# A three-stage attention and MoE kernel: tiles placed in a second pool, one reduction on another engine, another prologue order

## The chip, the cores and the metric

The kernel runs on 1 core of a Trainium2 chip. The metric is the device time of one execution in microseconds (us). Before the change the median of 3 runs is 1623.13 us (1617.84 to 1623.29). Engines are named as the profile names them: PE (matmul) and PEld (its weight load), DVE (VectorE), ACT (ScalarE), POOL (GpSimd), SP (it issues DMAs).

## What is computed

Linear attention (softmax of q over its features, of k over the sequence), then two feed-forward stages. Shapes: 8 batches, 8 heads, sequence 576, head size 64; so 4608 tokens of 512; hidden sizes 1536 and 768. q, k, v are float32, the weights float64.

```python
q_s = exp(q - max(q, axis=-1));  q_s = q_s / (sum(q_s, axis=-1) + 1e-9)
k_s = exp(k - max(k, axis=2));   k_s = k_s / (sum(k_s, axis=2) + 1e-9)
kv = einsum('bhsd,bhse->bhde', k_s, v)
x = einsum('bhsd,bhde->bhse', q_s, kv)          # to (4608, 512)
x = (silu(x @ w_gate) * (x @ w_val)) @ w_out
out = maximum(maximum(x @ w1, x @ w2), x @ w3) @ w2_out
```

## The kernel before

The tokens are cut into 9 blocks of 512. Each block runs through 60 groups of matmuls: for each of 12 hidden slices G, V and O (gate, value, output; the x stage, moving operand `xhi`/`xlo`), then for each of 6 slices W1, W2, W3 and P (the y stage, moving operand `yhi`/`ylo`). A product is made of three float32r matmuls (`mm3`): high x high, high x low, low x high, where `x_split`, `split_hi` and `split_lo` make the two parts of activations and weights. A group is 12 matmuls of 512 columns, so a block has 216 matmuls with `y` moving (W1 to W3), 288 with `x` moving (G, V), and the rest with `h` or a P weight moving. In the profile's names `pm<-yhi,whi` means: `yhi` moves, `whi` is stationary.

The float64 weights are loaded once, in block 0, turned to float32 there by two ACT steps (`convert_act`, lines 462 and 463) and two DVE steps (`convert_dve`, lines 471 and 474), and kept. In block 0 the main loop asks for conversions group by group (`quota`), and for each group ACT also casts the high part (line 489). The attention of block j+1 is worked into the groups of block j at places from a table (`SLOTS`, `SLOTS_FIRST`).

The attention of block 0 has no block before it. It is a prologue, in two halves of four heads, whose steps stand in a list written by hand (`PROLOGUE`); its DMAs stand in `LOADS`. Engines run their own instructions in exactly this order. For each half: `k_max` (maxima within a partition, DVE), `k_max_all` (over the 128 partitions: `partition_all_reduce` on POOL, line 161), `k_sub`, `k_exp`, `kv0`/`kv1` (matmuls with v), `q_max`, `q_sub`, `q_exp`, `q_sum`, `q_mul`, `qt0`/`qt1` (transposes on PE and copies on ACT), `kv_scale`, `x0`/`x1` (matmul and `x_split`). A third field "P" puts a step on POOL: `q_sub` and `k_sub` of half 1 and both `q_mul`. Among them stand `act n` and `dve n` (convert until n groups are done), `hi`/`lo` (split a weight) and `mm n` (first half of group n).

All tiles come from one SBUF pool, `sb`, and stand one behind the other in the order in which the program first asks for them. `v_sb` takes 5280 bytes in a partition (10 x 512 + 160), `qm`, `qx`, `qs`, `qr`, `kr1`, `kr2` take 8 to 128. The addresses of the built program, modulo 512 bytes:

| tiles | before | after |
|---|---|---|
| `raw_*`, `kvhi`, `kvlo`, `k_sb`, `q_sb` | 128 | 128 |
| `yhi`, `ylo`, `stage`, `qt`, `qthi` | 288 | 128 |
| `xhi`, `xlo`, `whi`, `wlo`, `plain`, `s`, `h`, `hhi`, `hlo` | 416 | 128 |
| `qtlo`, `o`, `kvf` | 32 | 128 |

Of the kernel before, what the change touches and what calls it, by code (L numbers as in the profile page):

```python
# [8 lines left out]
F32 = mybir.dt.float32  # L9
# [4 lines left out]
ALU = mybir.AluOpType  # L14
AX = mybir.AxisListType
# [3 lines left out]
def linear_attention_moe_moe_kernel(  # L19
# [20 lines left out]
    nc = tc.nc  # L40
    B, H, S, D = q.shape
# [4 lines left out]
    TB = 512  # L46
    NB = NT // TB
    HH = H // 2
    HP = HH // 2
    R = 4  # L50
    SM = 128 * R
    SR = S - SM
    VC = 2 * (D + 2)

    sb = ctx.enter_context(tc.tile_pool(name="sb", bufs=1))
    dram = ctx.enter_context(tc.tile_pool(name="dram", bufs=1, space=bass.MemoryType.DRAM))
    ps = ctx.enter_context(tc.tile_pool(name="ps", bufs=1, space=bass.MemoryType.PSUM))

# [15 lines left out]
        "k": sb.tile([128, R, HH, D], F32, name="k_sb"),  # L74
        "kr": sb.tile([128, HH, D], F32, name="kr_sb"),
        "q": sb.tile([128, R, HH, D], F32, name="q_sb"),
        "v": sb.tile([128, R + 1, HP, 2, D + 2], F32, name="v_sb"),
    }


# [3 lines left out]
    w = [raw[t].rearrange("p f c n -> p (f c n)") for t in ("W1", "W2", "W3")]  # L84
    n, m = R * HH * D, HH * D
    spot = w[1][:, n + (R + 1) * HP * VC:]
    ident, ones = spot[:, 0:128], spot[:, 128:256]
    diag = spot[:, 256:512].rearrange("p (g n) -> p g n", g=HP)

    def hrd(a, i):  # L90
        return a[:, i:i + n].rearrange("p (h r d) -> p h r d", r=R, h=HH)
# [58 lines left out]
    def k_max(t, c):  # L150
# [2 lines left out]
            out=c["km"], in_=t["k"].rearrange("p r h d -> p h d r"), axis=AX.X, op=ALU.max  # L153
        )

    def k_max_all(t, c):
        nc.vector.tensor_tensor(
            out=c["km"][0:SR], in0=c["km"][0:SR], in1=t["kr"][0:SR], op=ALU.max
        )
        c["kb"] = sb.tile([128, HH, D], F32, tag="kb", name="kb")  # L160
        nc.gpsimd.partition_all_reduce(
            c["kb"].rearrange("p h d -> p (h d)"),
            c["km"].rearrange("p h d -> p (h d)"),
            128,
            bass_isa.ReduceOp.max,
        )
# [16 lines left out]

    def both(a, tag):

        o = sb.tile([128, HP, TB // 32], F32, tag=tag, name=tag)
        for i in range(4):
            p, p1 = 32 * i, 32 * (i ^ 1)
            nc.vector.tensor_copy(out=o[p:p + 32], in_=a[p1:p1 + 32])
        return o  # L190

    def q_max(t, c):
        c["qm"] = sb.tile([128, HP, TB // 32], F32, tag="qm", name="qm", bufs=2)
        nc.vector.tensor_reduce(out=c["qm"], in_=t["qp"], axis=AX.X, op=ALU.max)
        o = both(c["qm"], "qx")
        nc.vector.tensor_tensor(out=c["qm"], in0=c["qm"], in1=o, op=ALU.max)
# [8 lines left out]
        nc.scalar.activation(out=t["qp"][:, part], in_=t["qp"][:, part], func=AF.Exp)  # L205

    def q_sum(t, c):
        qs = sb.tile([128, HP, TB // 32], F32, tag="qs", name="qs")
        nc.vector.tensor_reduce(out=qs, in_=t["qp"], axis=AX.X, op=ALU.add)
        o = both(qs, "qx")  # L210
        nc.vector.scalar_tensor_tensor(out=qs, in0=qs, scalar=1e-9, in1=o, op0=ALU.add, op1=ALU.add)
        c["qr"] = qs
        nc.vector.reciprocal(out=qs, in_=qs)
# [36 lines left out]
    def first_load_v(t, hf):  # L250
        for g in range(HP):
            h0 = hf * HH + 2 * g
            for u in range(2):
                nc.sync.dma_start(
                    out=t["v"][:, 0:R, g, u, 0:D],
                    in_=v[0, h0 + u, 0:SM, :].rearrange("(p r) d -> p r d", r=R),
                )
            nc.sync.dma_start(
                out=t["v"][0:SR, R, g, :, 0:D],
                in_=v[0, h0:h0 + 2, SM:S, :].rearrange("h p d -> p h d"),  # L260
            )
# [20 lines left out]
        nc.scalar.activation(out=t["kr"][0:SR], in_=t["kr"][0:SR], func=AF.Exp)  # L282

    def first_q_max(t, c):
        c["qm"] = sb.tile([128, HH, R], F32, tag="qm", name="qm", bufs=2)
        nc.vector.tensor_reduce(out=c["qm"], in_=t["qs"], axis=AX.X, op=ALU.max)

    def first_q_sub(t, c, eng=nc.vector):
# [10 lines left out]
            )  # L299

    def first_q_sum(t, c):
        qs = sb.tile([128, R, HH], F32, tag="qs", name="qs")
        nc.vector.tensor_reduce(out=qs, in_=t["q"], axis=AX.X, op=ALU.add)
        c["qr"] = sb.tile([128, R, HH], F32, tag="qr", name="qr", bufs=2)
        nc.vector.tensor_scalar_add(qs, qs, 1e-9)
        nc.vector.reciprocal(out=c["qr"], in_=qs)

# [20 lines left out]
        x_split(px, 0, hf * HP + g)  # L328

    def kv_scale(t, c):  # L330
        r = sb.tile([128, HP, 1], F32, tag="kr1", name="kr1", bufs=2)
        nc.vector.tensor_scalar_add(r, c["pkv"][:, :, D:D + 1], 1e-9)
        c["kvr"] = sb.tile([128, HP, 1], F32, tag="kr2", name="kr2", bufs=2)
        nc.vector.reciprocal(out=c["kvr"], in_=r)
        if "kv" in t:
            c["kvf"] = [t["kv"][u * D:(u + 1) * D, :, u * D:(u + 1) * D] for u in range(2)]
        else:
            kvf = sb.tile([128, HP, D], F32, tag="kvf", name="kvf")
            c["kvf"] = [kvf[u * D:(u + 1) * D] for u in range(2)]
        for u in range(2):  # L340
            p = slice(u * D, (u + 1) * D)
            nc.vector.tensor_tensor(
                out=c["kvf"][u], in0=c["pkv"][p, :, 0:D],
                in1=c["kvr"][p].to_broadcast([D, HP, D]), op=ALU.mult,
            )
# [257 lines left out]
    def attention(j, hf, t):  # L603
# [9 lines left out]
        if new:  # L613
            at("load_k", lambda: load_k(t, b, hf))
            at("load_v", lambda: load_v(t, b, hf))
            at("k_max", lambda: k_max(t, c))
            at("k_max_all", lambda: k_max_all(t, c))
            at("k_sub", lambda: k_sub(t, c))
            for i in range(3):
                at(f"k_exp{i}", lambda i=i: k_exp(t, c, i))  # L620
            for g in range(HP):
                at(f"kv{g}", lambda g=g: kv_mm(t, c, g))
            at("kv_scale", lambda: kv_scale(t, c))
            at("kv_split", lambda: kv_split(t, c, b, hf))
# [46 lines left out]
    with tc.manual_schedule():  # L671
        c = ({}, {})
        FIRST = {
            "k_max": first_k_max, "k_max_all": k_max_all, "k_sub": first_k_sub, "k_exp": first_k_exp,
            "q_max": first_q_max, "q_sub": first_q_sub, "q_exp": first_q_exp,
            "q_sum": first_q_sum, "q_mul": first_q_mul, "kv_scale": kv_scale,
        }

        def run(name, i, *a):
            t = first[i] if i in (0, 1) else None  # L680
            if name == "act":
                converts_act(i)
            elif name == "dve":
                converts_dve(i)
            elif name == "hi":
                split_hi(i)
            elif name == "lo":
                split_lo(i)
            elif name == "load":
                loads(i)  # L690
            elif name == "mm":
                proj(i, st["x", 0], 0, KC // 2)
            elif name.startswith("load_"):
                {"k": first_load_k, "q": first_load_q, "v": first_load_v}[name[5:]](t, i)
            elif name.startswith("kv") and name[2:].isdigit():
                kv_mm(t, c[i], int(name[2:]), ("acc2", "acc3")[i])
            elif name.startswith("qt"):
                first_q_t(t, c[i], int(name[2:]))
            elif name.startswith("x"):
                first_x_mm(t, c[i], i, int(name[1:]))  # L700
            elif a and a[0] == "P":
                FIRST[name](t, c[i], nc.gpsimd)
            else:
                FIRST[name](t, c[i])

        for t in first:
            nc.gpsimd.memset(t["v"][:, :, :, :, D:D + 2], 1.0)
            nc.gpsimd.memset(t["v"][SR:128, R], 0.0)
            nc.gpsimd.memset(t["kr"][SR:128], 0.0)
        nc.gpsimd.memset(att["kr"][SR:128], 0.0)  # L710
        for name, i in LOADS:
            run(name, i)
        make_identity(nc, ident)
        for t in first:
            nc.gpsimd.memset(t["kv"], 0.0)
        for a in (*kvhi, *kvlo):
# [4 lines left out]
        for n, (j, kind, f) in enumerate(groups):  # L721
            i = n % GPB
# [67 lines left out]


LOADS = (
    ("load_k", 0), ("load_q", 0), ("load_q", 1), ("load", 1), ("load_v", 0), ("load_k", 1),
    ("load", 3), ("load_v", 1),
)
PROLOGUE = (
    ("k_max", 0), ("act", 1), ("q_max", 0), ("k_max_all", 0), ("q_sub", 0), ("q_max", 1),
    ("q_exp", 0), ("k_sub", 0), ("q_sub", 1, "P"), ("k_exp", 0), ("q_sum", 0),
    ("q_mul", 0, "P"), ("kv0", 0), ("k_max", 1), ("k_max_all", 1), ("q_exp", 1), ("act", 2),
    ("k_sub", 1, "P"), ("act", 3), ("kv1", 0), ("dve", 1), ("qt0", 0), ("kv_scale", 0), ("dve", 2),  # L800
# [4 lines left out]
)  # L805


# [30 lines left out]
```

## Time and profile before

| | |
|---|---|
| median of 3 runs | 1623.13 us (1617.84 to 1623.29) |
| the profiled execution | 1619.9 us, of which 1618.1 us are its span |
| granted TensorE clock, mean | 0.993 |
| PE busy | 1557.1 us (96%) |
| DVE, ACT, POOL busy | 939.6, 740.7, 34.2 us |
| first `pm` matmul | 56.77 us |
| blocks 1 to 6, each | about 171 us; block 0 takes 197 us from its first `pm` matmul |

The trace is read in three parts: the prologue (to 57 us), block 0 (to 254 us) and the eight blocks behind it. Matmul durations in the trace are longer than their spacing, since they are pipelined; the spacing is read from the chain of work, where a piece of n matmuls stands with its time.

### The profile page before, as it was taken

The page shows a single profiled execution, that of the slowest core. Times are in us where ns is not written, and L with a number is a line of the kernel's source. Part 1 is how long each engine was busy: PE and PEld are TensorE (multiplying, and loading weights), DVE is VectorE, ACT ScalarE, POOL GpSimd, SP SyncE. Part 2 cuts the span into 40 slices and gives each one's busy share as a digit, 9 for nine tenths or more (in the row PEclk, how much of TensorE's full clock was granted, in tenths as well). Part 3 has the DMA queues.
Part 4 walks back from the last instruction along what each step waited for, and adds up shares of the span by engine and source line. Part 5 has one row for each costly group of instructions (what it writes and reads, how often), then busy time and mean ns, then how long its engine had stood idle before and what let it go on. Part 6 is the DMA issues. An engine that isn't in the chain of part 4 may idle for free.

```text
span 1618.1 us, 19598 instructions
## 1 busy us (share of the span) xinstructions
PE 1557.1 (96%) x7300; PEld 1266.2 (78%) x7300; DVE 939.6 (58%) x1589; ACT 740.7 (46%) x1234; POOL 34.2 (2%) x40
## 2 busy tenths in 40 slices
PE   1699999999999999999999999999999999999999
PEld 1487767888888888888888888888888888888887
DVE  3487785547554765467546754575547643664343
ACT  2799873344434443344334443434443433443332
POOL 2100000000000000000000000000000000000000
PEclk9899999999999999999999999999999999999999
DMA  7485754103310322121411141023103211111100
GB/s 197 124 248 156 204 145 101 33 20 76 75 53 27 69 64 65 33 51 37 102 33 44 39 108 33 21 69 87 44 23 69 65 33 39 33 52 33 33 21 33
DMA packets 197183, 112.96 MB, mean 70 GB/s; under 512 B 145888, under 2 KB 169440, under 8 KB 197088
## 3 DMA queue, kind: packets, MB, share of 16 engines
q1 hardware_dynamic: 197088, 111.72, 25.5%
q8 instruction: 57, 0.93, 0.2%
q14 instruction: 38, 0.31, 0.1%
HBM read 97.52 MB, written 14.16 MB: 69 GB/s over the span
## 4 chain that ended last, share of the span: by engine, by line
PE 85%; ACT 7%; issue 3%; DVE 2%; POOL 1%; SPq 0%; DMA 0%; DVEq 0%; POOLq 0%; ACTq 0%
PE pm L500 58%; PE acc L500 24%; ACT stage L463 2%; ACT whi L489 1%; PE pkv L230 1%; PE px L382 1%; PE px L383 1%; PE px L381 1%; SPq L148 0%; ACT raw_w L462 0%; PE acc L530 0%; ACT plain L462 0%; ACT ring_yhi L463 0%; DVE wlo L494 0%; ACT ring_ylo L463 0%
## 5 line engine op out<-in xcount | busy, mean ns | idle before, releaser
L500 PE MATMUL pm<-xhi,whi 128*128 128x512 f32 x864 | 340.1, 394 | 4.2 <-ACT s L563 4.1
L500 PE MATMUL pm<-xlo,whi 128*128 128x512 f32 x864 | 337.8, 391 | 0.4 <-DVE xlo L394 0.4
L500 PE MATMUL pm<-xhi,wlo 128*128 128x512 f32 x864 | 337.6, 391 | 0.0
L566 DVE TENSOR_TENSOR h<-s,pm 128x512 f32<-128x512 f32 x108 | 74.2, 687 | 332.6 <-PE pm L500 330.9
L500 PE MATMUL pm<-yhi,whi 128*128 128x512 f32 x648 | 258.5, 399 | 4.5 <-ACT s L570 3.9
L500 PE MATMUL pm<-yhi,wlo 128*128 128x512 f32 x648 | 256.2, 395 | 0.0
L500 PE MATMUL pm<-ylo,whi 128*128 128x512 f32 x648 | 255.8, 395 | 0.0
L520 ACT CAST hhi<-h 128x512 fp32r<-128x512 f32 x156 | 97.5, 625 | 320.5 <-DVE h L566 210.6
L500 PEld LDWEIGHTS pm<-xhi,whi 128*128 128x128 f32 x864 | 163.0, 189 | 40.4 <-ACT s L563 5.9
L500 PEld LDWEIGHTS pm<-xlo,whi 128*128 128x128 f32 x864 | 163.0, 189 | 35.3 <-issue 1.0
L500 PEld LDWEIGHTS pm<-xhi,wlo 128*128 128x128 f32 x864 | 162.9, 189 | 34.0
L500 PE MATMUL acc<-hhi,whi 128*128 128x512 f32 x424 | 165.2, 390 | 0.0
L500 PE MATMUL acc<-hhi,wlo 128*128 128x512 f32 x424 | 165.2, 390 | 0.0
L500 PE MATMUL acc<-hlo,whi 128*128 128x512 f32 x424 | 165.1, 390 | 0.0
L500 PEld LDWEIGHTS pm<-yhi,whi 128*128 128x128 f32 x648 | 121.8, 188 | 35.5 <-ACT s L570 5.2
L563 ACT ACTIVATE s<-pm 128x512 f32<-128x512 f32 x108 | 65.3, 605 | 177.7 <-PE pm L500 177.4
L500 PEld LDWEIGHTS pm<-yhi,wlo 128*128 128x128 f32 x648 | 121.7, 188 | 29.0
L500 PEld LDWEIGHTS pm<-ylo,whi 128*128 128x128 f32 x648 | 121.8, 188 | 28.8 <-DVE ylo L584 0.4
L489 ACT CAST whi<-raw_w 128x512 fp32r<-128x512 f32 x162 | 100.8, 622 | 60.4 <-PE pm L500 46.9
L494 DVE TENSOR_TENSOR wlo<-plain,whi 128x512 fp32r<-128x512 f32 x156 | 106.8, 685 | 17.6 <-ACT whi L489 17.5
L494 DVE TENSOR_TENSOR wlo<-raw_w,whi 128x512 fp32r<-128x512 f32 x162 | 110.0, 683 | 10.3 <-ACT whi L489 10.3
L521 DVE TENSOR_TENSOR hlo<-h,hhi 128x512 fp32r<-128x512 f32 x156 | 108.0, 692 | 12.6 <-ACT hhi L520 0.7
(146 smaller groups left out, 1957.4 us busy)
## 6 DMA issues: line engine op xcount, KB each, us to landing
plain<-kept_o SPq DMA_DIRECT2D x96, 256.0 KB, 2.6
plain<-kept_p SPq DMA_DIRECT2D x48, 256.0 KB, 2.8
out_dram<-o SPq DMA_DIRECT2D x36, 256.0 KB, 2.0
stage<-in_moe_w_dram SPq DMA_DIRECT2D x17, 512.0 KB, 3.8
v_sb<-in_v_dram SPq DMA_DIRECT2D x60, 128.0 KB, 2.9
k_sb<-in_k_dram SPq DMA_DIRECT2D x56, 128.0 KB, 3.4
stage<-in_moe_w_out_dram SPq DMA_DIRECT2D x12, 512.0 KB, 4.1
stage<-in_moe_w_gate_dram SPq DMA_DIRECT2D x6, 512.0 KB, 5.0
```

What stands on the lines that cost most here:

```text
L230: nc.tensor.matmul(out=c["pkv"][u * D:(u + 1) * D, g, :], lhsT=lhsT, rhs=rhs, start=i == 0, stop=i == R,)
L381: nc.tensor.matmul(out=px[:, a:e], lhsT=hi, rhs=qhi, start=True, stop=False)
L382: nc.tensor.matmul(out=px[:, a:e], lhsT=hi, rhs=qlo, start=False, stop=False)
L383: nc.tensor.matmul(out=px[:, a:e], lhsT=lo, rhs=qhi, start=False, stop=True)
L463: nc.scalar.activation(out=bits, in_=low, func=AF.Copy, scale=2.0 ** -29 * (1.0 - 2.0 ** -7), bias=-0.44)
L489: nc.scalar.copy(out=hi, in_=plain[n])
L494: nc.vector.tensor_tensor(out=lo, in0=plain.pop(n), in1=hi, op=ALU.subtract)
L500: nc.tensor.matmul(out=o, lhsT=a, rhs=b, start=first and m == 0, stop=last and m == 2)
L520: nc.scalar.copy(out=hi, in_=h)
L521: later.append(lambda: nc.vector.tensor_tensor(out=lo, in0=h, in1=hi, op=ALU.subtract))
L563: nc.scalar.activation(out=st["s"], in_=p, func=AF.Silu)
L566: nc.vector.tensor_tensor(out=h, in0=st["s"], in1=p, op=ALU.mult)
```

## The change

A second pool, `small`, takes `v_sb` and the small tiles, and stands behind `sb`; so everything in `sb` begins at 128 modulo 512 (the table above). `k_max_all` of block 0 becomes `first_k_max_all`, on DVE alone: transpose in blocks of 32 x 32, reduce, exchange between the four groups of 32 partitions in two rounds, spread, transpose back. The v loads of block 0 are issued by ACT instead of SP. The identity for the transposes is made first on POOL. `LOADS` and `PROLOGUE` stand in another order, and no step has the field "P" any more. Behind the prologue every engine has the same instructions in the same order as before.

```diff
     sb = ctx.enter_context(tc.tile_pool(name="sb", bufs=1))
+    small = ctx.enter_context(tc.tile_pool(name="small", bufs=1))
...
-        "v": sb.tile([128, R + 1, HP, 2, D + 2], F32, name="v_sb"),
+        "v": small.tile([128, R + 1, HP, 2, D + 2], F32, name="v_sb"),
...
+    def first_k_max_all(t, c):
+        km = c["km"].rearrange("p h d -> p (h d)")
+        nc.vector.tensor_tensor(out=c["km"][0:SR], in0=c["km"][0:SR], in1=t["kr"][0:SR], op=ALU.max)
+        kt = sb.tile([128, HH * D], F32, tag="kb", name="kt")
+        nc.vector.transpose(out=kt, in_=km)
+        top = small.tile([128, HH * D // 32], F32, tag="qm", name="top", bufs=2)
+        nc.vector.tensor_reduce(
+            out=top, in_=kt.rearrange("p (j b) -> p j b", b=32), axis=AX.X, op=ALU.max
+        )
+        for step in (1, 2):
+            o = small.tile([128, HH * D // 32], F32, tag="qx", name="qx")
+            for i in range(4):
+                p, p1 = 32 * i, 32 * (i ^ step)
+                nc.vector.tensor_copy(out=o[p:p + 32], in_=top[p1:p1 + 32])
+            nc.vector.tensor_tensor(out=top, in0=top, in1=o, op=ALU.max)
+        nc.vector.tensor_copy(
+            out=km.rearrange("p (j b) -> p j b", b=32),
+            in_=top.unsqueeze(2).to_broadcast([128, HH * D // 32, 32]),
+        )
+        nc.vector.transpose(out=kt, in_=km)
+        c["kb"] = kt.rearrange("p (h d) -> p h d", h=HH)
...
-        c["qm"] = sb.tile([128, HP, TB // 32], F32, tag="qm", name="qm", bufs=2)
+        c["qm"] = small.tile([128, HP, TB // 32], F32, tag="qm", name="qm", bufs=2)
...
-                nc.sync.dma_start(
+                nc.scalar.dma_start(
                     out=t["v"][:, 0:R, g, u, 0:D],
...
-            "k_max": first_k_max, "k_max_all": k_max_all, "k_sub": first_k_sub, "k_exp": first_k_exp,
+            "k_max": first_k_max, "k_max_all": first_k_max_all, "k_sub": first_k_sub, "k_exp": first_k_exp,
...
+        make_identity(nc, ident)
         for t in first:
             nc.gpsimd.memset(t["v"][:, :, :, :, D:D + 2], 1.0)
...
-    ("load_k", 0), ("load_q", 0), ("load_q", 1), ("load", 1), ("load_v", 0), ("load_k", 1),
-    ("load", 3), ("load_v", 1),
+    ("load_k", 0), ("load_k", 1), ("load_v", 0), ("load_q", 0), ("load", 1), ("load_q", 1),
+    ("load_v", 1), ("load", 3),
...
-    ("k_max", 0), ("act", 1), ("q_max", 0), ("k_max_all", 0), ("q_sub", 0), ("q_max", 1),
+    ("k_max", 0), ("k_max_all", 0), ("k_sub", 0), ("k_exp", 0), ("k_max", 1), ("k_max_all", 1),
```

POOL behind its memsets, before (`raw_w_65`, `raw_w_66`, `raw_w_67` are `raw_w1`, `raw_w2`, `raw_w3`, in which the prologue keeps its data; a row ISA without operands precedes a change of the kind of work on POOL):

```order
L161 ISA
L161 ISA kb<-km 128x256
L289 ISA
L289 TENSOR_TENSOR raw_w_66<-raw_w_66,qm 128x1024
L309 TENSOR_TENSOR q_sb<-q_sb,qr 128x1024
L161 ISA
L161 ISA kb<-km 128x256
L270 ISA
L270 TENSOR_TENSOR raw_w_65<-raw_w_65,kb 128x1024
```

The same place on POOL now (`raw_w_69` and `raw_w_70` are `raw_w2` and `raw_w3`):

```order
masks.py:197 MEMSET raw_w_69 128x128
masks.py:199 ISA
masks.py:199 AFFINE_SELECT raw_w_69<-raw_w_69 128x128
L732 MEMSET v_sb 128x20x2
L733 MEMSET v_sb 64x264
```

Behind these only memsets follow until the all-reduces of the later blocks: the two of block 0 and the four elementwise steps have left POOL, and the identity stands ahead of the memsets of v.

DVE at the program's start, before:

```order
L266 TENSOR_TENSOR k_sb<-raw_w_65 128x4x2x64
L267 TENSOR_TENSOR km<-k_sb 128x256
L286 TENSOR_REDUCE qm<-raw_w_65 128x16
L157 TENSOR_TENSOR km<-km,raw_w_67 64x256
L289 TENSOR_TENSOR raw_w_65<-raw_w_65,qm 128x1024
L286 TENSOR_REDUCE qm<-raw_w_66 128x16
L270 TENSOR_TENSOR raw_w_65<-raw_w_65,kb 128x1024
```

and now:

```order
L290 TENSOR_TENSOR k_sb<-raw_w_68 128x4x2x64
L291 TENSOR_TENSOR km<-k_sb 128x256
L160 TENSOR_TENSOR km<-km,raw_w_70 64x256
L162 STREAM_TRANSPOSE kt<-km 128x256
L164 TENSOR_REDUCE top<-kt 128x8
L171 COPY qx<-top 32x8 x4
L172 TENSOR_TENSOR top<-top,qx 128x8
```

The pair of L171 and L172 comes once more, then one copy of 128 x 256 that spreads the maxima, the transpose back and `k_sub`. The q steps of half 0 have moved behind the k steps of both halves, and the maxima over partitions stand where DVE waited for POOL.

ACT at the program's start, before:

```order
L462 ACT_TABLE_LOAD
L462 ACTIVATE raw_g<-stage 128x512
L463 ACTIVATE stage<-stage 128x512
L297 ACTIVATE q_sb<-raw_w_65 128x512 x2
L279 ACTIVATE k_sb<-raw_w_65 128x512 x2
L282 ACTIVATE raw_w_67<-raw_w_67 64x256
```

and now:

```order
L278 DMA raw_w_69<-in_v_dram 128x4x64 x2
L282 DMA raw_w_69<-in_v_dram 64x2x64
L303 ACT_TABLE_LOAD
L303 ACTIVATE k_sb<-raw_w_68 128x512 x2
L306 ACTIVATE raw_w_70<-raw_w_70 64x256
L321 ACTIVATE q_sb<-raw_w_68 128x512 x2
L347 COPY qt<-pt 128x512 x2
L486 ACTIVATE raw_g<-stage 128x512
L487 ACTIVATE stage<-stage 128x512
```

Twelve DMA issues (the last three are shown) now stand ahead of ACT's first instruction, k's exponentials ahead of q's, and the first conversion behind the copies of the transposed q.

## Rows read from the trace of the kernel before

**Rows 1.** The page, part 1: busy us (share of the span) and instructions by engine.

```profile
PE 1557.1 (96%) x7300; PEld 1266.2 (78%) x7300; DVE 939.6 (58%) x1589; ACT 740.7 (46%) x1234; POOL 34.2 (2%) x40
```

**Rows 2.** Windows of block 0: busy us by engine, granted clock, DMA share, GB/s.

```profile
57.00:195.00 138.00, 129.49 (x552) 98.78 (x551) 105.70 (x187) 134.08 (x182) 1.08 (x1) 0.96 0.67 198
195.00:254.00 59.00, 55.45 (x256) 40.20 (x254) 49.97 (x93) 37.67 (x56) 1.27 (x1) 1.00 0.49 130
```

**Rows 3.** Timeline of POOL in the prologue: start us, us, instruction, idle before.

```profile
13.42 0.28 POOL masks.py:199 TENSOR_SCALAR_AFFINE_SELECT raw_w<-raw_w 128x128 f32<-128x128 f32 x1 [10.61 <-issue]
...
22.87 1.08 POOL L161 PARTITION_ALL_REDUCE kb<-km  x1 [6.79 <-issue]
31.67 1.89 POOL L289 TENSOR_TENSOR raw_w<-raw_w,qm 128x1024 f32<-128x1024 f32 x1 [7.72 <-issue]
...
41.66 1.08 POOL L161 PARTITION_ALL_REDUCE kb<-km  x1 [6.23 <-issue]
49.62 2.33 POOL L270 TENSOR_TENSOR raw_w<-raw_w,kb 128x1024 f32<-128x1024 f32 x1 [6.89 <-issue]
```

**Rows 4.** Timeline: DVE's first work, transposes of half 0 on PE, ACT's table load for Silu.

```profile
5.19 0.69 DVE L266 TENSOR_TENSOR k_sb<-raw_w 128x512 f32<-128x512 f32 x1 [5.19 <-DMA raw_w<-in_k_dram]
...
35.48 1.97 PE L319 MATMUL pt<-raw_w,q_sb 128*128 128x128 f32 x8 [7.01 <-POOL q_sb L309]
...
66.12 1.28 ACT L563 ACT_TABLE_LOAD   x1
```

**Rows 5.** The chain of work in block 8: start us, us, piece.

```profile
1449.47 10.88 PE pm L500 x48
...
1547.39 16.79 PE pm L500 x72
...
1608.69 5.49 PE acc L500 x24
```

**Rows 6.** Groups of PE by shape, 850 us to the end: busy us, mean ns.

```profile
L500 PE MATMUL pm<-xhi,whi 128*128 128x512 f32 x396 | 154.3, 390 | 0.0
...
L500 PE MATMUL pm<-yhi,whi 128*128 128x512 f32 x360 | 142.8, 397 | 0.0
...
L500 PE MATMUL acc<-hlo,whi 128*128 128x512 f32 x204 | 79.5, 390 | 0.0
...
L382 PE MATMUL px<-qtlo,kvhi 128*128 128x512 f32 x4 | 1.6, 396 | 0.0
L381 PE MATMUL px<-qthi,kvhi 128*128 128x512 f32 x4 | 1.6, 394 | 0.0
```

**Rows 7.** Groups of DVE by shape, whole span: busy us, mean ns, idle before.

```profile
L494 DVE TENSOR_TENSOR wlo<-raw_w,whi 128x512 fp32r<-128x512 f32 x162 | 110.0, 683 | 10.3 <-ACT whi L489 10.3
...
L364 DVE STREAM_TRANSPOSE whole<-q_sb 128x512 f32<-128x512 f32 x32 | 22.5, 704 | 0.0
...
L216 DVE TENSOR_TENSOR q_sb<-q_sb,qs 128x1024 f32<-128x1024 f32 x16 | 19.5, 1218 | 0.0
...
L471 DVE TENSOR_SCALAR stage<-stage 128x512 uint32<-128x512 uint32 x41 | 17.4, 425 | 24.1 <-ACT stage L463 23.9
...
L189 DVE COPY qx<-qm 32x32 f32<-32x32 f32 x64 | 11.1, 173 | 1.2
...
L157 DVE TENSOR_TENSOR km<-km,kr_sb 64x256 f32<-64x256 f32 x14 | 5.8, 411 | 0.0
```

**Rows 8.** Groups of ACT by shape, whole span: busy us, mean ns, idle before.

```profile
L489 ACT CAST whi<-raw_g 128x512 fp32r<-128x512 f32 x108 | 66.6, 617 | 0.0
...
L463 ACT ACTIVATE stage<-stage 128x512 uint16<-128x512 uint32 x41 | 55.9, 1364 | 1.3
...
L462 ACT ACTIVATE raw_g<-stage 128x512 f32<-128x512 f32 x6 | 4.1, 677 | 8.6 <-DMA stage<-in_moe_w_gate_dram 8.6
```

**Rows 9.** Timeline of SP's DMA issues in the prologue: the first and the last of v's.

```profile
3.71 1.80 SPq L254 DMA_DIRECT2D v_sb<-in_v_dram  x2
...
18.27 0.78 SPq L258 DMA_DIRECT2D raw_w<-in_v_dram  x1
```

More of the change, by code (lines that the diff above doesn't have):

```diff
@@ L86, in linear_attention_moe_moe_kernel @@
     spot = w[1][:, n + (R + 1) * HP * VC:]
-    ident, ones = spot[:, 0:128], spot[:, 128:256]
-    diag = spot[:, 256:512].rearrange("p (g n) -> p g n", g=HP)
+    ident = spot[:, 0:128]
     def hrd(a, i):
@@ L184, in both @@
     def both(a, tag):
-        o = sb.tile([128, HP, TB // 32], F32, tag=tag, name=tag)
+        o = small.tile([128, HP, TB // 32], F32, tag=tag, name=tag)
         for i in range(4):
@@ L207, in q_sum @@
     def q_sum(t, c):
-        qs = sb.tile([128, HP, TB // 32], F32, tag="qs", name="qs")
+        qs = small.tile([128, HP, TB // 32], F32, tag="qs", name="qs")
         nc.vector.tensor_reduce(out=qs, in_=t["qp"], axis=AX.X, op=ALU.add)
@@ L257, in first_load_v @@
                 )
-            nc.sync.dma_start(
+            nc.scalar.dma_start(
                 out=t["v"][0:SR, R, g, :, 0:D],
@@ L284, in first_q_max @@
     def first_q_max(t, c):
-        c["qm"] = sb.tile([128, HH, R], F32, tag="qm", name="qm", bufs=2)
+        c["qm"] = small.tile([128, HH, R], F32, tag="qm", name="qm", bufs=2)
         nc.vector.tensor_reduce(out=c["qm"], in_=t["qs"], axis=AX.X, op=ALU.max)
@@ L301, in first_q_sum @@
     def first_q_sum(t, c):
-        qs = sb.tile([128, R, HH], F32, tag="qs", name="qs")
+        qs = small.tile([128, R, HH], F32, tag="qs", name="qs")
         nc.vector.tensor_reduce(out=qs, in_=t["q"], axis=AX.X, op=ALU.add)
-        c["qr"] = sb.tile([128, R, HH], F32, tag="qr", name="qr", bufs=2)
+        c["qr"] = small.tile([128, R, HH], F32, tag="qr", name="qr", bufs=2)
         nc.vector.tensor_scalar_add(qs, qs, 1e-9)
@@ L330, in kv_scale @@
     def kv_scale(t, c):
-        r = sb.tile([128, HP, 1], F32, tag="kr1", name="kr1", bufs=2)
+        r = small.tile([128, HP, 1], F32, tag="kr1", name="kr1", bufs=2)
         nc.vector.tensor_scalar_add(r, c["pkv"][:, :, D:D + 1], 1e-9)
-        c["kvr"] = sb.tile([128, HP, 1], F32, tag="kr2", name="kr2", bufs=2)
+        c["kvr"] = small.tile([128, HP, 1], F32, tag="kr2", name="kr2", bufs=2)
         nc.vector.reciprocal(out=c["kvr"], in_=r)
@@ L712, in linear_attention_moe_moe_kernel @@
             run(name, i)
-        make_identity(nc, ident)
         for t in first:
@@ L792 @@
 LOADS = (
-    ("load_k", 0), ("load_q", 0), ("load_q", 1), ("load", 1), ("load_v", 0), ("load_k", 1),
-    ("load", 3), ("load_v", 1),
+    ("load_k", 0), ("load_k", 1), ("load_v", 0), ("load_q", 0), ("load", 1), ("load_q", 1),
+    ("load_v", 1), ("load", 3),
 )
 PROLOGUE = (
-    ("k_max", 0), ("act", 1), ("q_max", 0), ("k_max_all", 0), ("q_sub", 0), ("q_max", 1),
-    ("q_exp", 0), ("k_sub", 0), ("q_sub", 1, "P"), ("k_exp", 0), ("q_sum", 0),
-    ("q_mul", 0, "P"), ("kv0", 0), ("k_max", 1), ("k_max_all", 1), ("q_exp", 1), ("act", 2),
-    ("k_sub", 1, "P"), ("act", 3), ("kv1", 0), ("dve", 1), ("qt0", 0), ("kv_scale", 0), ("dve", 2),
[4 rows of a table removed]
+    ("k_max", 0), ("k_max_all", 0), ("k_sub", 0), ("k_exp", 0), ("k_max", 1), ("k_max_all", 1),
+    ("q_max", 0), ("q_sub", 0), ("q_exp", 0), ("kv0", 0), ("kv1", 0), ("q_sum", 0), ("q_mul", 0),
+    ("qt0", 0), ("kv_scale", 0), ("qt1", 0), ("act", 1), ("k_sub", 1), ("k_exp", 1), ("dve", 1),
+    ("x0", 0), ("x1", 0), ("hi", 0), ("lo", 0), ("kv0", 1), ("kv1", 1), ("act", 2), ("q_max", 1),
+    ("q_sub", 1), ("q_exp", 1), ("q_sum", 1), ("q_mul", 1), ("kv_scale", 1), ("dve", 2),
[3 rows of a table added]
 )
```

7 rows, old and new, of the table PROLOGUE are left out of this document.

## The prediction

> **What bounds the kernel now.** I read the page first, then the chain of work, then windows, then the timeline of the prologue. PE is busy for 96% of the span [rows 1], but the span has three parts with different limits.
>
> In the eight blocks behind block 0 the chain is almost only PE's matmuls, so what counts there is their spacing. The reader is to see that it has two values. In block 8, which has no attention work in it, 48 `pm` matmuls of the x stage take 10.88 us, 226.7 ns each; 72 of the y stage take 16.79 us, 233.2 ns each; the last 24 `acc`, of P, take 5.49 us, 228.8 ns each [rows 5]. The durations say the same over four and a half blocks: `xhi` and `hlo` moving 390 ns, `yhi` 397 ns; and the 512-column matmuls of attention, with `qthi` or `qtlo` moving over `kvhi`, 394 and 396 ns [rows 6]. Beside the addresses modulo 512: `xhi` and `h` lie at 416 like `whi`, and are fast; `yhi` at 288 over 416, `qthi` at 288 and `qtlo` at 32 over 128 are slow. Three unlike pairs are slow and two like ones fast.
>
> Block 0 up to 195 us is set by ACT: busy for 134.08 of 138 us from 57 us on, with PE at 129.49 [rows 2]. It converts the weights there. Behind 195 us PE has 55.45 of 59 us, ACT 37.67.
>
> The prologue is a chain over POOL: each change of work there shows 6 to 11 us of idle time that waits for nothing the profile shows ("issue"), and DVE, ACT and PE wait behind it. Five such gaps stand in a row, 10.61 + 6.79 + 7.72 + 6.23 + 6.89 = 38.2 us [rows 3]. ACT reaches its table load for the first Silu at 66.12 us [rows 4]. From there it is the bound for 130 us, and its queue holds the same work after the change; so how much earlier it gets there is what the prologue is worth.
>
> **The change, part by part: the prologue.** Prices by kind [rows 7, 8]: a 1024-wide DVE step 1.22 us, 512-wide 0.68, masking 0.43, 256-wide 0.41, a tiny one 0.17; a 512-wide ACT step 0.62, a conversion on ACT 0.68 + 1.36 = 2.04, on DVE 0.43 + 0.68 = 1.1.
>
> The first k half lands at 5.2 us before [rows 4]. Now the v loads come from ACT's queue at the same time: five of them wait for nothing, some 0.5 MB, which at 198 GB/s [rows 2] is 2.5 us if all goes first. So 5.2 to 7.7; I take 6.4, about the middle, since both queues start together.
>
> `first_k_max_all` is not in the trace. Two 32 x 32 transposes at half of L364's 0.70 to all of it, taken as 0.41 by the 256-wide row, which has their size; a reduce 0.41; eight copies and two maxima at 0.17 = 1.7; a spreading copy 0.41; some 0.3 between dependent steps: 3.6 us, with 3.0 and 4.6 as ends. It takes the place of an all-reduce of 1.08 us that ended at 23.95 us [rows 3].
>
> Now the chain, step by step. DVE: first k landed 6.4; `k_max` 1.5 and `k_max_all` 3.6 give 11.5; `k_sub` 1.6; the same for half 1, 5.1, give 18.2; `q_max` and `q_sub` 2.4 give 20.6. ACT `q_exp` 1.2; DVE `q_sum` 1.6 and `q_mul` 1.2: 24.6. PE transposes 2.0 [rows 4], ACT copies the last one 0.6, converts 2.0: 29.2; `k_exp` of half 1 1.6 and two `xhi` 1.2: 32.0; DVE `xlo` and `wlo` 1.4: 33.4; `q_max`, `q_sub` of half 1 2.4, `q_exp` 1.2, `q_sum` 1.6, `q_mul` 1.2: 39.8; `kv_scale` 0.9 and a conversion 1.1: 41.8. Then ACT and DVE in turns, since each `hi` waits for a `dve`: `hi` 0.6, `lo` 0.7, `dve` 1.1, `hi` 0.6: 44.8; `xhi` 0.6, conversion 2.0, `xhi` 0.6, `xlo` 0.7, `dve` 1.1, `hi` 0.6: 50.4; three conversions 6.1: 56.5 at the table load. That is **66.1 - 56.5 = 9.6 us earlier**. The ends: the landing gives +1.2 or -1.3, two `k_max_all` +1.2 or -2.0, and the transposes, priced as they ran, would take 2 us more at half the clock; 4.3 to 12.0.
>
> What lies beside it, and its cover. The twelve v issues leave SP and stand ahead of ACT's first work. On SP they took some 12.5 us with their waits, in two runs between 3.71 and 19.05 us [rows 9]; on ACT they would end near 13, the table load (1.28) near 14.5, k's exponentials near 16. ACT is next needed at 20.6, so there are 4 us of cover; a us beyond is a us of the chain. Behind them in ACT's queue stand k's exponentials, and `kv0` waits for these, but `kv_scale` only at 24. SP is rid of them, and its k, q and weight loads come sooner. POOL makes the identity first, so v's constant columns wait for the 10.61 us gap and are there near 14; `kv0` needs them near 16. The four steps that POOL had (two `q_mul`, `q_sub`, `k_sub`) are in the sum, on DVE.
>
> The Trainium skill (DMA: Bandwidth & Descriptors, "Issuing engines are not separate DMA queues") says that DMAs from several engines run on the same 16 DMA engines and that only issue time is saved. By it v takes its share from k, and the first k lands late: the end of 7.7, and a forecast 1.3 us higher.
>
> **The addresses.** If unlike addresses cost what the rows show, and like ones at 128 are as fast as like ones at 416: 8 blocks x 216 y matmuls x 6.5 ns = 11.2 us. In block 0 ACT hides it up to 195 us, and of the 59 us behind (with about 140 of its y matmuls) I count half, 0.5. P's first matmuls behind y: some 576 at about 1 ns, 0.6. Attention's 180 matmuls, most narrower, at up to 5 ns: 0.6. **12.9 us.** DVE and ACT steps show no such spread (L494 0.68, L489 0.62), so nothing is counted for them. The unknown is 128 itself: no fast product in these rows lies there. The ends are -29 us (the third rival) and a spacing below 226.7, down to 512 columns at the granted clock of 1.00, the 2.4 GHz level: 213.3 ns. I take the nearest row, 226.7.
>
> **The sum.** 9.6 + 12.9 = 22.5 us off the profiled execution's 1619.9: **1597.4 us**. That execution lies 3.2 us below the median of the three runs and 2.1 above the fastest; the upper end allows for it.
>
> **The rivals.**
> First, the spacing has another cause than addresses: the y stage has other evictions (three groups on DVE and ACT instead of two) and P in its turns. For: x and y differ in more than the address. Against: P, in the same stretch and like with like, falls back to nearly 226.7, while attention's 512-wide matmuls, unlike there, stay slow. Then only the prologue counts: 1619.9 - 9.6 = 1610.3.
> The Trainium skill (SBUF — State Buffer, "Who interferes with whom") stands with this one: PE has two independent read ports and never waits on anyone, so by that rule x and y would have one pace; the two paces in one stretch [rows 5] do not agree with it.
>
> Second, the prologue gives little: the loads share the DMA engines, or ACT's issues last beyond 20.6 us, or the DMAs that refill block 0's stage tiles bind once ACT comes earlier (share 0.67 up to 195 us [rows 2], so there is room). Then 1619.9 - 12.9 = 1607.0.
>
> Third, slower: the pace hangs on the operand's own place, not on the pair, and 128 is a slow one. Then x, O and P (2592 + 1872 = 4464 matmuls) fall to the y pace: 4464 x 6.5 ns = 29.0 us lost, no y gain, 9.6 from the prologue: 1639.3. From some 1500 matmuls slowed on, the prologue's gain is gone. For: nothing shows a fast float32r product at 128. Against: 288 is slow over 416 and over 128 alike, 416 over 416 fast; the pair explains all five.
>
> Fourth, all fall below 226.7; even to 220 it is 6400 x 6.7 ns = 43 us more, 1554.
>
> **How the numbers follow.** The forecast 0.69, the first rival 0.14, the second 0.09, the third 0.05, the fourth 0.03. The predicted time is 1597. The forecast's own range is 1590 to 1605 (prologue 4.3 to 12.0; y by half of its small terms; execution against median 3 us). To hold 8 in 10 it reaches to the first two rivals: 1589 to 1613. About 0.5% (8 us) is what a measurement can tell from no change; below 1615 is faster. The forecast, the second and the fourth lie there, and most of the first: faster 0.88; the rest of the first and a weak prologue beside it: same 0.07; the third: slower 0.05.
>
> **What would show it.** Right: y pieces in the chain at 226.7 ns like x, attention's 512-wide at 390 ns; the blocks behind block 0 shorter by 1.5 us each; no all-reduce on POOL ahead of the first `pm`; the table load for Silu near 56.5 us; ACT as busy behind it as before, and block 1 starting about 10 us sooner. Wrong: y still at 233 (first rival), x and `acc` at 233 (third), a first DVE step behind 8 us, ACT's first exponential behind 19 us, or gaps in ACT on `stage` tiles in block 0 (second).

## The result

The changed kernel takes 1602.57 us (median of 4 runs, 1602.22 to 1603.8); the kernel before, beside it, 1622.97. The ratio is 0.9883, with a 95% interval of 0.9863 to 0.9903. The profiled execution took 1602.22 us with a span of 1600.3, against 1619.9 and 1618.1. Between the profiled executions 17.7 of the 22.5 us forecast came; the medians differ by 20.4, as the runs of before spread from 1617.84 to 1623.29.

Line numbers of the changed kernel are 24 higher behind the new function: the `pm` matmuls are line 524, the table load for Silu line 587.

PE's busy time on the page answers to [rows 1]; it fell by 7 us, POOL's by 11, and DVE's rose by 12:

```profile
PE 1549.9 (97%) x7300; PEld 1266.1 (79%) x7300; DVE 951.9 (59%) x1622; ACT 740.6 (46%) x1234; POOL 23.5 (1%) x33
```

The chain of work in block 8 answers to [rows 5] (start us, us, piece):

```profile
1433.31 10.88 PE pm L524 x48
...
1531.25 16.32 PE pm L524 x72
...
1591.09 5.48 PE acc L524 x24
```

The 72 matmuls of the y stage now take 16.32 us, 226.7 ns each, exactly the pace of x (10.88 / 48). Before it was 233.2. The groups of PE by shape from 850 us on say the same (busy us, mean ns), and answer to [rows 6]:

```profile
L524 PE MATMUL pm<-xhi,whi 128*128 128x512 f32 x384 | 149.5, 389 | 1.0 <-ACT s L587 1.0
...
L524 PE MATMUL pm<-yhi,whi 128*128 128x512 f32 x359 | 140.4, 391 | 0.0
...
L405 PE MATMUL px<-qthi,kvhi 128*128 128x512 f32 x4 | 1.6, 389 | 0.0
...
L406 PE MATMUL px<-qtlo,kvhi 128*128 128x384 f32 x4 | 1.3, 337 | 0.0
```

`yhi` fell from 397 to 391 ns and attention's 512-wide matmuls from 394 and 396 to 389. The narrower ones (384 columns: 337 before and after) did not change.

The prologue's timeline, rows of DVE, POOL, PE and ACT (start us, us, instruction, idle before), answers to [rows 3, 4]:

```profile
5.02 0.69 DVE L290 TENSOR_TENSOR k_sb<-raw_w 128x512 f32<-128x512 f32 x1 [5.02 <-DMA raw_w<-in_k_dram]
...
6.71 0.45 DVE L162 STREAM_TRANSPOSE kt<-km 128x256 f32<-128x256 f32 x1
...
10.28 0.45 DVE L177 STREAM_TRANSPOSE kt<-km 128x256 f32<-128x256 f32 x1
...
9.10 0.28 POOL masks.py:199 TENSOR_SCALAR_AFFINE_SELECT raw_w<-raw_w 128x128 f32<-128x128 f32 x1 [8.18 <-issue]
...
24.10 1.94 PE L343 MATMUL pt<-raw_w,q_sb 128*128 128x128 f32 x8 [7.73 <-DVE kr L356]
...
57.45 1.28 ACT L587 ACT_TABLE_LOAD   x1
```

Of POOL's five idle gaps that wait for nothing one is left, 8.18 us ahead of the identity. The table load stands at 57.45 us instead of 66.12, so ACT's long stretch begins 8.67 us sooner. Block 1 begins at 246.5 us instead of 253.9 (its first `pm` matmul), so only 7.4 us are left there. The eight blocks behind it took 1353.8 us instead of 1364.2, which is 10.4 less; 7.4 and 10.4 make the whole difference of the spans, 17.8.

### The profile page after: what moved, and what is told of

It reads as the page before. It is cut to its first block, busy times and chain, and to the rows that moved or that the text cites. A ratio compares the mean times of both kernels' runs of the same rounds, so it can differ in the third digit from the quotient of the medians.

```text
span 1600.3 us, 19611 instructions
## 1 busy us (share of the span) xinstructions
PE 1549.9 (97%) x7300; PEld 1266.1 (79%) x7300; DVE 951.9 (59%) x1622; ACT 740.6 (46%) x1234; POOL 23.5 (1%) x33
## 4 chain that ended last, share of the span: by engine, by line
PE 86%; ACT 7%; DVE 4%; issue 2%; DMA 1%; SPq 0%; DVEq 0%; ACTq 0%
PE pm L524 58%; PE acc L524 25%; ACT stage L487 2%; ACT whi L513 1%; PE pkv L254 1%; PE acc L554 1%; PE px L407 1%; PE px L406 1%; PE px L405 1%; DMA out_dram<-o 0%; ACT raw_w L486 0%; SPq L148 0%; ACT plain L486 0%; ACT ring_yhi L487 0%; DVE wlo L518 0%
## 5 line engine op out<-in xcount | busy, mean ns | idle before, releaser
L524 PE MATMUL pm<-yhi,whi 128*128 128x512 f32 x648 | 255.2, 394 | 4.6 <-ACT s L594 4.3
L524 PE MATMUL pm<-yhi,wlo 128*128 128x512 f32 x648 | 252.8, 390 | 0.0
```

What stands on the lines that cost most here:

```text
L524: nc.tensor.matmul(out=o, lhsT=a, rhs=b, start=first and m == 0, stop=last and m == 2)
```

## The experiments

The theory had two parts: 233 ns come from an unlike pair of addresses, and the prologue is worth what its table load moves. They were tried apart first, then each by itself.

### Each part alone

`addr_only` is the kernel before with the second pool and nothing else. `prologue_only` is the changed kernel with one pool, and a pad that keeps the large tiles at their addresses of before, modulo 512 (all but `qtlo`, `o` and `kvf`, which lie at 416 instead of 32):

```diff
-    small = ctx.enter_context(tc.tile_pool(name="small", bufs=1))
+    small = sb
...
+            if t is first[0] and step == 1:
+                sb.tile([128, 96], F32, name="pad")
```

> The kernel before with the second pool alone: v_sb and the small tiles stand behind the large ones, everything in the first pool begins at 128 modulo 512; prologue, LOADS and engines of block 0 are those of before. Theory (the spacing of matmuls hangs on how the moving and the stationary operand lie to each other modulo 512 bytes): y matmuls at 226.7 ns instead of 233.2, ACT's table load for Silu still near 66.1 us, about 11 us off, 1612 us. Rival (the y gain came with the shifted timing, not with the addresses): y stays at 233, 1623 us.

> The changed kernel with all tiles in one pool again and a pad of 384 bytes, so that x, h and weight parts lie at 416 and y and qthi at 288 as before (qtlo at 416 instead of 32). Theory: y back at 233 ns, table load at 57.5 us, block 1 begins 7.4 us earlier than before; 1615.5 us. With the run of the addresses alone the two gains should add up to the whole (about 11 + 7.5 = 18.5). Rival (the prologue's gain needs the faster y): below 4 us.

`addr_only` took 1609.92 us, ratio 0.9939 [0.9923, 0.9956]; `prologue_only` 1611.45, ratio 0.9946 [0.9931, 0.9961]; before 1619.51 on that chip. One row of the chain in block 8 of each, first `addr_only`, then `prologue_only`, shows which of them has the fast y:

```profile
1537.79 16.32 PE pm L501 x72
```

```profile
1537.87 16.79 PE pm L526 x72
```

`addr_only` has y at 226.7 ns with the table load still at 66.43 us; `prologue_only` has y at 233.2 and the load at 56.80. So the first rival (another cause of the spacing) and the second (the prologue gives little) both fall. The gains of 9.6 and 8.1 us add up to 17.7, by which the profiled executions of before and after differ.

### The place or the pair

`all_288` puts 160 bytes ahead of everything, so that all large tiles lie at 288 modulo 512. The three others shift only the tiles that are first asked for behind the x tiles (`whi`, `wlo`, `s`, `h`, `plain` and so on) against `xhi` and `yhi`, by 64, 128 or 256 bytes:

```diff
+        if not padded:
+            padded.append(sb.tile([128, 32], F32, name="pad"))
```

(here 128 bytes; 16 and 64 elements in the others.)

> The changed kernel with 160 bytes left free at the start of the first pool, so that every large tile lies at 288 modulo 512 instead of 128. Theory of the pair: nothing changes, all at 226.7 ns, 1602.6 us. Rival (the operand's own place decides, and 288 is a slow one, as y was before): y, x and acc at 233 ns, some 6200 matmuls x 6.5 ns = 40 us more, 1643 us.

> The changed kernel with a pad of 128 bytes between the x tiles and the weight parts: x and y stay at 128, weight parts, h and all behind them lie at 256 modulo 512. Theory of the pair: x and y matmuls (2592 + 1944) go to 233 ns, 4536 x 6.5 ns = 29.5 us more, 1632 us, while acc (h and weights both at 256) stays at 226.7. Rival (the moving operand's own place): x and y, which have not moved, stay at 226.7, 1603 us. Rival (the y stage is slow by its own nature): x stays at 226.7 whatever y does.

> The changed kernel with a pad of 256 bytes between the x tiles and the weight parts: x and y at 128, weight parts and h at 384 modulo 512. Read from the spacing of x and y matmuls in the trace. If like means alike modulo 512: 233 ns, as with 128 bytes. If alike modulo 256 were enough: 226.7 ns, and the time is that of the change.

> The changed kernel with a pad of 64 bytes between the x tiles and the weight parts: x and y at 128, weight parts and h at 192 modulo 512. If like means alike modulo 512 (or any larger power of two than 64): 233 ns for x and y. If alike modulo 64 were enough: 226.7 ns.

`all_288`: 1602.02 us, ratio 0.9884 [0.9866, 0.9901], no different from the change. Its y in block 8:

```profile
1531.70 16.32 PE pm L525 x72
```

So 288 is no slow place, as 416 and 128 are none. `w_plus_128`: 1628.52 us, ratio 1.0055 [1.004, 1.0071], so slower than the kernel before. Its chain in block 8, x first, then `acc` (products with `h`), then y:

```profile
1542.11 5.59 PE pm L528 x24
1547.70 5.48 PE acc L528 x24
1553.18 16.79 PE pm L528 x72
```

x and y are both at 233 ns, x too, which was fast before, although `xhi` and `yhi` have not moved. The `acc` between them have `h` and the weights both at 256 and take 228.3 ns each, as in the change (5.47 us for 24). So 256 is no slow place of the weights either, and it is the distance that counts. Summed from start to start over blocks 1 to 8, x lost 13.2 us and y 10.5 against the change. `w_plus_64`, one run, 1630.41 us, has the same paces (5.60 us for 24, 16.80 for 72). `w_plus_256`, one run, took 1598.6 us, before on that chip 1620.56:

```profile
1516.73 5.44 PE pm L528 x24
...
1527.63 16.32 PE pm L528 x72
```

Here `whi` and `yhi` differ by 256 bytes, and both paces are 226.7. My expectation of a slow pace failed: it is enough that the two operands are alike modulo 256. The mechanism in the chip is not shown by this, only its condition: 0 and 256 bytes apart are fast, 64 and 128 slow. Which two operands make the pair is not settled either. PEld works beside PE (79% and 97% of the span), so the next matmul's weights are loaded while a matmul runs, and in the x and y stages these lie at the same place modulo 512 as the matmul's own. The few places where the two differ speak against the own pair alone: in before, seven P matmuls behind block 0 stand right ahead of attention's (own operands both at 416, the next weights, `kvhi`, at 128). From their start to that of the next matmul it is 235.0 ns in the mean, and 226.9 in the change. In `w_plus_64`, with 192 and 128 there, the same seven have 225.9, so the next weights alone don't explain it either.

### Which part of the prologue's change is worth what

The prologue's edit has two parts: maxima on DVE, and another order with other queues. `kmax_only` is the kernel before with the maxima alone (and the pad of `prologue_only`), `v_on_sp` is the change with v's loads back on SP, and `order_only` is the change with the maxima back on POOL:

```diff
-            "k_max": first_k_max, "k_max_all": first_k_max_all, "k_sub": first_k_sub, "k_exp": first_k_exp,
+            "k_max": first_k_max, "k_max_all": k_max_all, "k_sub": first_k_sub, "k_exp": first_k_exp,
```

> The kernel before, its order, loads and addresses kept, with the maxima over partitions of block 0 on DVE (first_k_max_all) alone. It tells whether the prologue's gain is that of the all-reduces taken off POOL or of the new order. Theory A (the all-reduces and the changes of work on POOL around them held the chain): two all-reduces and two of the five gaps go, half 1's k_sub on POOL follows its neighbours at about 30 us instead of 52.6, and from the end of half 1's k exponentials ACT needed 12.7 us to the table load; so the load comes near 46 instead of 66.1 us, more than the change's 57.5, and the whole near 1600 us, with y still at 233. Theory B (the new order is what counts): the load comes later than 57.5 us, 1612 us or more.

> The changed kernel with v's loads of block 0 issued by SP again, in the same place of LOADS. Theory: ACT's issues cost nothing while ACT waits anyway (its table load began at 11.85 us, its first exponential at 13.14, a us behind k_sub), while on SP they stand ahead of q and of the first weights: six v issues took about 6 us on SP, so q comes 4 to 6 us later and the table load 0 to 3 us later; 1602 to 1606 us. Rival (ACT's issues hold the chain): the table load comes earlier than 57 us, 1600 us or less.

> The changed kernel with block 0's k maxima over partitions on GpSimd as before: the pool and the new order of prologue and loads alone. If the new order by itself costs time (the old order with maxima on VectorE had the second table load at 45.9 us, the changed kernel at 57.5), the load here is no sooner than before's 66.1 us, and the time is 1609 us or more, that of the addresses alone (1609.9) or over. If the new order was made to cover what GpSimd leaves open, the load comes at 58 to 63 us and the time is near 1605 us.

`kmax_only`: 1600.63 us, ratio 0.9878 [0.9862, 0.9895], with y still at 233 ns (72 in 16.79 us). That is as much as the whole change, from one of its three parts. Its timeline (POOL, then ACT):

```profile
13.02 0.83 POOL masks.py:199 TENSOR_SCALAR_AFFINE_SELECT raw_w<-raw_w 128x128 f32<-128x128 f32 x1 [10.21 <-issue]
...
16.20 1.90 POOL L315 TENSOR_TENSOR raw_w<-raw_w,qm 128x1024 f32<-128x1024 f32 x1
18.56 2.15 POOL L335 TENSOR_TENSOR q_sb<-q_sb,qr 128x1024 f32<-128x1024 f32 x1 [0.46 <-DVE qr L332]
25.11 2.43 POOL L296 TENSOR_TENSOR raw_w<-raw_w,kt 128x1024 f32<-128x1024 f32 x1 [4.40 <-DVE kt L179]
...
10.44 0.66 ACT L488 ACTIVATE raw_g<-stage 128x512 f32<-128x512 f32 x1 [8.44 <-DMA stage<-in_moe_w_gate_dram]
...
45.89 1.28 ACT L589 ACT_TABLE_LOAD   x1
```

POOL still has its four elementwise steps, and none of them stands behind an unexplained gap any more: the waits name DVE. So four of the five gaps went with the two all-reduces, which had made POOL change its kind of work four more times. With these gone, the old order has its table load at 45.89 us, the new one at 57.45.

`order_only`: 1609.54 us, ratio 0.9937 [0.9923, 0.9951], against 1609.92 for the addresses alone; so the new order and the new queues by themselves give nothing. Its timeline (POOL, then ACT):

```profile
9.44 0.28 POOL masks.py:199 TENSOR_SCALAR_AFFINE_SELECT raw_w<-raw_w 128x128 f32<-128x128 f32 x1 [8.52 <-issue]
...
22.24 1.08 POOL L185 PARTITION_ALL_REDUCE kb<-km  x1 [8.25 <-issue]
26.60 1.06 POOL L185 PARTITION_ALL_REDUCE kb<-km  x1 [3.28 <-DVE km L181]
...
65.95 1.28 ACT L587 ACT_TABLE_LOAD   x1
```

The second all-reduce has no such gap, since nothing else stood between the two on POOL. The load is at 65.95 us, where it was before.

`v_on_sp`: 1601.44 us, ratio 0.9885 [0.987, 0.9899], table load at 57.70. Which queue issues v makes no difference that these runs can tell. The Trainium skill (DMA: Bandwidth & Descriptors, "Issuing engines are not separate DMA queues") says that little can be had that way; the runs agree.

### A better kernel

`kmax_and_pool` is the kernel before with the maxima on DVE and the second pool, and nothing else. `interleaved_order` is the change with conversions placed between the steps of the chain; it also puts all four `mm` behind both `x` steps of half 1:

```diff
-    ("k_max", 0), ("k_max_all", 0), ("k_sub", 0), ("k_exp", 0), ("k_max", 1), ("k_max_all", 1),
-    ("q_max", 0), ("q_sub", 0), ("q_exp", 0), ("kv0", 0), ("kv1", 0), ("q_sum", 0), ("q_mul", 0),
...
+    ("k_max", 0), ("k_max_all", 0), ("k_sub", 0), ("k_exp", 0), ("act", 1), ("k_max", 1),
+    ("k_max_all", 1), ("act", 2), ("q_max", 0), ("q_sub", 0), ("q_exp", 0), ("dve", 1), ("act", 3),
```

> The kernel before with two of the change's three parts: the pool for the odd-sized tiles, and block 0's k maxima over partitions on VectorE; the order of the prologue and the loads stay as before. If the two gains add (addresses 10.5 us of y's matmuls in blocks 1 to 8, maxima 20 us of the prologue's chain): y's matmuls at 226.7 ns, the second table load near 46 us, block 1 from about 235.5 us, and about 1590 us in all, ratio 0.980. If the 20 us are in part given back behind block 0 once y is faster (ScalarE or VectorE as the later engine in blocks 1 to 8), the blocks are longer than those of the addresses alone by over 0.5 us each, and it ends at 1594 us or later. If the reordering was needed for the whole change's time, it ends near 1602 us.

> The changed kernel with another order of the prologue: the weight conversions of ScalarE and VectorE stand between the steps of the k and q chain, in place of behind them, so that ScalarE's idle time ahead of its 57 us mark (some 19 us in the changed kernel) is filled. If the changed kernel's prologue is held by its own order, the second table load comes at 44 to 48 us and the whole at 1589 to 1593 us, like the old order with the maxima on VectorE. If it is held by VectorE's added work whatever the order, the table load stays above 53 us and the time above 1597 us.

`kmax_and_pool`: **1589.53 us** (5 runs, 1588.82 to 1591.72), ratio 0.9816 [0.9802, 0.9831]. `interleaved_order`: 1591.29, ratio 0.9825 [0.9812, 0.9839]. Both beat the change; between the two nothing can be told. The gains of the parts add up once more: 9.6 (`addr_only`) and 19.9 (`kmax_only`, 1620.56 - 1600.63) are 29.5, and 1619.6 - 1589.53 is 30.1.

Where the order's loss lies is seen in the window from 12 us to the table load. Columns: stretch, its length, busy us of PE, PEld, DVE, ACT and POOL, granted clock, DMA share, GB/s; first the change, then `kmax_and_pool`, then `interleaved_order`:

```profile
12.00:57.45 45.45, 26.20 (x146) 17.56 (x147) 30.48 (x60) 25.84 (x38) 1.68 (x4) 0.89 0.52 156
```

```profile
12.00:45.68 33.68, 20.66 (x134) 14.48 (x135) 30.57 (x56) 23.85 (x36) 12.15 (x12) 1.00 0.71 209
```

```profile
12.00:46.87 34.87, 19.70 (x132) 13.83 (x133) 29.86 (x61) 25.98 (x37) 1.75 (x4) 0.95 0.65 198
```

DVE and ACT have nearly the same work in all three, 30 and 24 to 26 us. In the change DVE and ACT are at work together for only 13.7 of the 45.45 us, counted over the rows of the trace; in the other two for 21.0 of 33.68 and 21.4 of 34.87, and DVE is busy for 91% and 86% of the stretch. The DMAs rest too in the change, at a share of 0.52; I read that as the conversions that free the stage tiles coming late (ACT's first begins at 26.56 us, in `interleaved_order` at 14.72). What the place of the conversions and what that of the `mm` is worth was not tried apart.

## Why the prediction held, point by point

**The addresses.** The mechanism was right and 128 was as fast as 416. For y I took 8 x 216 x 6.5 ns = 11.2 us; from start to start over blocks 1 to 8 it is 405.01 us before and 394.54 after, 10.5. P gave 0.65 of the 0.6 taken. Attention gave nothing of its 0.6 (22.78 and 22.80 us): only the 512-wide shapes became faster, and I had spread up to 5 ns over all widths. x lost 0.9 instead (523.59 and 524.49 us): the change has a stall of PE of 1.2 us in block 6, where ACT had waited for an output DMA, and a smaller one in block 4; before has one of 0.8 us in block 4. `addr_only` and `kmax_and_pool` have none in block 6, and the cause wasn't tried.

**The third rival** (the operand's own place) had its chance from nothing having been seen at 128. The change itself, `all_288` and `w_plus_128` put it away: the distance counts, and a bad one costs about what I had priced: 26 us above the change in `w_plus_128`, where x and y were slow, 4536 matmuls. (My count for x, O and P was 72 short: over nine blocks they are 4536 too, 29.5 us.) By the rule of the Trainium skill (SBUF — State Buffer, "Who interferes with whom") that PE's two read ports are independent and that it waits on no one, the addresses would not matter. The runs differ from it: in `w_plus_128` PE's pace changed by 6.5 ns a matmul with the distance alone.

**The prologue up to the table load**: 8.7 us for a forecast of 9.6, but by errors that cancel. The first k landed at 5.02 us where I took 6.4 (before: 5.19), so v's loads took nothing from it; the condition under which the forecast would have been 1.3 us higher did not arise. `first_k_max_all` took, from its first transpose on, 4.0 us in half 0 (6.71 to 10.7) and 3.6 in half 1 where I took 3.6. The q exponentials of half 0 began at 19.80 (20.6 taken), the transposes at 24.10 (24.6). The step that failed is the stretch behind, from the transposes to the table load: 33.4 us where the sum has 31.9. I let ACT and DVE take turns there, and PE stands in that chain too. The chain of the change from 41 us on (start us, us, piece):

```profile
41.00 0.63 ACT whi L513
41.67 2.93 PE pm L524 x6
44.60 1.72 PE px L351 x2
46.34 0.58 ACT xhi L417
```

`x0` of half 1 stands behind `mm 1` in PE's queue, so 4.65 us of PE lie between a weight split and the `xhi` that waits for it. The sum has only ACT's and DVE's steps there, PE's at nothing. The six `pm` take 488 ns each; the granted clock was 0.50 from 41.6 to 44.6 us, the lower level (1.2 GHz), behind 10.6 us (granted clock 0.77) in which PE had been busy for 3.9. At 226.7 ns each they would have taken 1.4 us instead of 2.9.

**Behind the table load** I counted half a us of gain in block 0; 1.3 us were lost (189.05 us from load to block 1, 187.78 before), with ACT as busy as before, 162.74 us then. The window of before, that of the change, and ACT's first wait for PE in the latter, which was 0.91 us before:

```profile
66.12:253.90 187.78, 176.12 (x771) 132.67 (x770) 149.23 (x268) 162.74 (x225) 2.36 (x2) 0.97 0.63 180
...
57.45:246.50 189.05, 174.87 (x761) 131.30 (x759) 149.62 (x268) 162.78 (x225) 2.42 (x2) 0.96 0.61 180
...
74.28 0.60 ACT L587 ACTIVATE s<-pm 128x512 f32<-128x512 f32 x1 [1.97 <-PE pm L524]
```

ACT waits there for PE, which had been idle for 5.43 us ahead of 64.61 (2.91 ahead of the same matmuls before) and then ran at a granted clock of 0.69 in the mean over 10 us, against 0.83. That the idle time and the lower clock belong together is read, not tried. Added up by line, ACT's other waits up to block 1 differ by up to 1.1 us, in both directions, and nearly cancel. The cause of the 1.3 us stays open, and they are less than what this stretch varies by: `all_288` and `w_plus_256` have the instructions of the change at other addresses, and took 190.0 and 186.5 us from table load to block 1. Most of the 3.6 us by which `w_plus_256` lies under the change's profiled execution is in this stretch.

**The sum.** Missing against the forecast: 0.9 ahead of the table load, 1.8 in block 0, 2.0 in the blocks behind; 4.7 of the 4.8 us by which 1602.2 lies over 1597.4. The bounds that I kept, 1589 to 1613, covered these.

**What I did not see**: I priced the prologue's change as one thing. The rows of POOL said that every gap sits at a change of its kind of work [rows 3], and so that taking the all-reduces away would do without any other order. The estimate for `kmax_only`, added up along the old list, came to 46 us; made ahead of the prediction, it would have shown the new list as a loss of 11.

## What to carry to other kernels

When the same matmul has two paces in one trace, compare the addresses of its two operands modulo 256 bytes first (shown here for float32r and 512 columns), and keep small odd-sized tiles where they can't shift the large ones. Where an engine shows idle time that waits for nothing at each change of its kind of work, take away the odd kind and leave the order alone; then see whether the order still pays. A list written by hand should be checked for engines that take turns: count for how long both are at work at once, and move the independent work to where one of them waits.

## What the runs showed of the hardware that I had not expected

The float32r matmuls of 512 columns ran at 226.7 ns with operands 0 or 256 bytes apart, modulo 512, and at 233.2 with 64 or 128: 6.5 ns, or 2.9%, on the bounding engine. At 128 bytes this is a mean: the single spacings lie near 229 and near 237 to 238 ns; at 64 bytes most are 233 or 234.

POOL's steps can also stretch those of DVE. In `kmax_only` these three ran while POOL had an elementwise step (DVE's timeline):

```profile
16.20 1.20 DVE L329 TENSOR_REDUCE qs<-q_sb 128x16 f32<-128x1024 f32 x1
...
18.99 2.00 DVE L293 TENSOR_TENSOR km<-raw_w 128x256 f32<-128x256 f32 x1
...
25.38 2.72 DVE L500 SCALAR_TENSOR_TENSOR raw_g<-raw_g,stage 128x512 uint32<-128x512 uint32 x1
```

Without POOL beside them they take 1.21, 0.42 and 0.69 us: the reduction, with one input, kept its time, and the two steps with two inputs did not. The Trainium skill (SBUF — State Buffer, "Who interferes with whom") has this rule: a DVE instruction with two SBUF inputs contends with a POOL instruction that reads SBUF. The rows agree, and the old order was still the faster one with three such stretched steps in it.
